# Two row tiles of x: transposed by DMA in place of TensorE

## The chip, the cores and the metric

The kernel runs on one core of a Trainium2 chip. The metric is the device time of one execution in microseconds, and the number to compare is the median of several executions. One further execution is taken with the hardware profiler; every duration, start and wait in this document is from such a profile, with times counted from the start of its span. In the profile PE is TensorE (PEld its weight loads), DVE VectorE, ACT ScalarE, POOL GpSimd, and SP is SyncE, whose queue issues every DMA of this kernel.

## The reference: what is computed

For x of 2048 rows and 1024 columns (bf16) the kernel computes a mix of two branches:

```python
g = sigmoid((x * gate_w).sum(-1))
# branch a: 32 heads of 32, each position attends 8 positions, 2 apart
q, k, v = x @ wqkv
o = softmax(scale * q . k[pos - 2*w], w = 0..7) . v
a = o @ wo
# branch b: gated MLP with mixing over the positions, Fh = 1792
z = gelu(x @ w_in);  z1, z2 = z[:, :Fh], layernorm(z[:, Fh:])
b = (z1 * (w_sp @ z2 + b_sp)) @ w_out
out = g * a + (1 - g) * b
```

Both branches start with a product over the columns of x. TensorE sums over the partition axis, so x is needed with its columns on the partitions: transposed.

## The kernel before

The 2048 rows are 16 tiles of 128 rows. `xT` holds x transposed, 128 partitions by 8 k tiles by 2048 rows, in one arena of SBUF that the whole kernel shares. The kernel goes through these stages, in this order on PE: six warm-up matmuls on zeros; a first block of `z2` (the second half of z) for row tiles 0 and 1 and the first two blocks of 448 columns of `w2`, the part of w_in that z2 needs (32 matmuls, L370); `z2` tiles 2 to 7 for the first block of columns, one more for the second; then the q, k, v projections of head group 0 (16 tiles of 8 matmuls, `qkv_tile`, L938), those of the other seven groups, with further z2 work between them, z1 (L1089), the mixing over the positions, and the two output products (L1106 for all three).

ACT empties the PSUM banks: gelu for z2 (L379), a copy into a staging slot for q, k, v (L941). Every fourth q/k/v tile SP stores the slot to DRAM (L946); there are three slots, so the fourth use of a slot waits for its store. Per head group the attention runs on DVE (L505 to L579), on q, k and v that SP loads back from DRAM in another layout (L587 to L596).

x reaches `xT` in two ways. Row tiles 0 and 1 are loaded as they lie (L915), into `xn`, a part of the arena that the attention uses later; `turn` transposes them on PE, four 128x128 pieces into one PSUM tile (L352), and ACT (L355) or DVE (L357) copies the PSUM tile to `xT`. Row tiles 2 to 15 are loaded by a transposing DMA, which writes straight into `xT` (L919, L922). `x_abs` (L383) sums the absolute values of two row tiles on DVE, for a scale that x is converted with later.

The order on each engine is the order in which the program gives the instructions. At the start that order is written out by hand. Later a planner (`Beat`) counts PE columns as time and puts DVE, ACT and DMA work in at due times; that is fixed when the kernel is built. SP is one queue: at the start it issues, in this order, the two plain x loads, eight loads of `w2` (one per k tile, 224 KB each), six transposed x loads, three loads of wqkv for group 0, eight transposed x loads, some small ones, wqkv for group 1, four loads of another part of w_in, and only then the first stores of q, k, v.

PSUM tiles are given out in turn: `bank()` takes every fourth from a pool of two, the others from a pool of six, from which `turn` takes its four too.

## Time and profile before

| | us |
|---|---|
| median of 3 runs (lowest, highest) | 672.64 (672.32, 672.66) |
| the profiled execution, its own time | 671.37 |
| span of that profile | 669.6 |
| PE busy in the span | 663.5 |
| DVE busy | 575.2 |
| ACT busy | 441.6 |
| moved by DMA | 123.92 MB, 185 GB/s on average |

The profile is of one execution, whose own time is 1.27 us below the median; the span leaves out 1.8 us around it. A busy PE is not a PE at its peak, since matmuls overlap and their ends are modelled. In a line of the timeline the columns are start, duration, engine, line, operation, what is written and read, and in brackets the idle time before it with what ended it. SPq is SP's queue: the duration there is the time that SP needs to issue the DMA, not the transfer.

### The profile page before, as it was taken

The page shows a single profiled execution, that of the slowest core. Times are in us where ns is not written, and L with a number is a line of the kernel's source. Part 1 is how long each engine was busy: PE and PEld are TensorE (multiplying, and loading weights), DVE is VectorE, ACT ScalarE, POOL GpSimd, SP SyncE. Part 2 cuts the span into 40 slices and gives each one's busy share as a digit, 9 for nine tenths or more (in the row PEclk, how much of TensorE's full clock was granted, in tenths as well). Part 3 has the DMA queues.
Part 4 walks back from the last instruction along what each step waited for, and adds up shares of the span by engine and source line. Part 5 has one row for each costly group of instructions (what it writes and reads, how often), then busy time and mean ns, then how long its engine had stood idle before and what let it go on. Part 6 is the DMA issues. An engine that isn't in the chain of part 4 may idle for free.

```text
span 669.6 us, 9598 instructions
## 1 busy us (share of the span) xinstructions
PE 663.5 (99%) x3564; PEld 389.8 (58%) x3564; DVE 575.2 (86%) x660; ACT 441.6 (66%) x774; POOL 9.4 (1%) x68
## 2 busy tenths in 40 slices
PE   9999999999999999999999999999999999999998
PEld 4568876666777777555555455555555544444443
DVE  4667999989999999999999999999978788954745
ACT  4437667788889989889754568777777774522122
POOL 0000000000001000000000000000000000000000
PEclk9999999999999999999999999999999999999999
DMA  8999574354298996994956686648589799476211
GB/s 237 176 246 269 103 203 131 91 121 119 49 278 250 281 303 186 277 342 146 276 209 217 140 216 162 159 123 231 141 209 287 144 242 253 93 159 150 56 63 64
DMA packets 229919, 123.92 MB, mean 185 GB/s; under 512 B 191088, under 2 KB 217456, under 8 KB 229872
## 3 DMA queue, kind: packets, MB, share of 16 engines
q1 hardware_dynamic: 229872, 123.31, 69.8%
q8 instruction: 28, 0.46, 0.3%
q14 instruction: 19, 0.16, 0.1%
HBM read 63.97 MB, written 37.82 MB: 152 GB/s over the span
## 4 chain that ended last, share of the span: by engine, by line
PE 55%; DVE 40%; ACT 3%; issue 2%; DVEq 0%; ACTq 0%
PE ps L1106 36%; DVE arena L509 8%; DVE arena L505 7%; DVE arena L572 7%; PE seed L1106 6%; PE ps L938 6%; DVE arena L578 3%; PE ps L370 2%; DVE arena L801 2%; PE sd L938 2%; DVE arena L579 2%; DVE arena L819 2%; DVE arena L575 1%; DVE att_L L512 1%; PE sd L370 1%
## 5 line engine op out<-in xcount | busy, mean ns | idle before, releaser
L1106 PE MATMUL ps<-arena 128*128 128x448 f16 (+1 forms) x1296 | 263.7, 363 | 0.7 <-ACT arena L1118 0.6
L1106 PEld LDWEIGHTS <-arena 128*128 128x128 f16 x1519 | 148.5, 98 | 155.0 <-issue 1.5
L938 PEld LDWEIGHTS <-arena 128*128 128x128 f16 (+1 forms) x1024 | 141.4, 138 | 30.6 <-issue 1.1
L938 PE MATMUL ps<-arena 128*128 128x384 bf16 x800 | 142.5, 326 | 0.7 <-DVE arena L487 0.7
L1089 PEld LDWEIGHTS <-arena 128*128 128x128 f16 x512 | 50.0, 98 | 46.6
L509 DVE TENSOR_TENSOR arena<-arena 128x4096 bf16<-128x4096 bf16 (+1 forms) x64 | 74.0, 1157 | 1.8
L1089 PE MATMUL ps<-arena 128*128 128x448 bf16 x384 | 75.4, 352 | 0.0
L505 DVE TENSOR_TENSOR arena<-arena 128x8192 bf16<-128x8192 bf16 x16 | 70.8, 4422 | 4.4 <-DMA arena<-k_d 4.1
L572 DVE TENSOR_TENSOR arena<-arena,att_A 128x8192 bf16<-128x8192 bf16 x16 | 70.7, 4420 | 0.2
L941 ACT CAST arena<-ps 128x384 bf16<-128x384 f32 x100 | 47.8, 487 | 29.4 <-PE ps L938 28.7
L1106 PE MATMUL seed<-arena 128*128 128x448 f16 (+2 forms) x223 | 48.7, 360 | 0.0
L370 PE MATMUL ps<-arena 128*128 128x448 bf16 x216 | 45.4, 352 | 0.2 <-ACT arena L355 0.2
L451 PE MATMUL ps<-arena 128*128 128x449 f16 x192 | 42.3, 353 | 0.0
L938 PE MATMUL sd<-arena 128*128 128x384 bf16 x224 | 41.0, 326 | 0.0
L1092 ACT ACTIVATE arena<-ps,x_sc 128x448 bf16<-128x448 f32 x48 | 29.5, 639 | 15.5 <-PE ps L1089 11.9
L1330 ACT ACTIVATE arena<-ps,omr 128x512 f32<-128x512 f32 x24 | 16.5, 687 | 32.7 <-PE ps L1106 32.7
L370 PEld LDWEIGHTS <-arena 128*128 128x128 f16 (+1 forms) x256 | 24.9, 98 | 22.0 <-ACT arena L355 0.5
L578 DVE TENSOR_TENSOR arena<-arena 128x4096 bf16<-128x4096 bf16 x16 | 36.6, 2287 | 0.2
L1264 DVE SCALAR_TENSOR_TENSOR arena<-seed,omr,arena 128x512 bf16<-128x512 f32 x8 | 6.0, 751 | 32.7 <-PE seed L1106 32.7
L451 PEld LDWEIGHTS <-arena 128*128 128x128 f16 x224 | 21.9, 98 | 18.1 <-issue 0.5
L760 ACT ACTIVATE arena<-arena 128x2048 bf16<-128x2048 bf16 x16 | 30.9, 1929 | 0.0
L885 ACT ACTIVATE arena<-arena 128x896 bf16<-128x896 bf16 x32 | 30.3, 947 | 0.5
(190 smaller groups left out, 738.4 us busy)
## 6 DMA issues: line engine op xcount, KB each, us to landing
arena<-in_B_w_sp_dram SPq DMA_DIRECT2D x16, 512.0 KB, 4.1
arena<-v_d SPq DMA_DIRECT2D x8, 960.0 KB, 6.6
z_d<-arena SPq DMA_DIRECT2D x16, 448.0 KB, 4.5
arena<-z_d SPq DMA_DIRECT2D x16, 448.0 KB, 3.6
y_d<-arena SPq DMA_DIRECT2D x16, 448.0 KB, 3.0
arena<-k_d SPq DMA_DIRECT2D x7, 960.0 KB, 7.3
arena<-in_A_wqkv_dram SPq DMA_DIRECT2D x24, 256.0 KB, 4.7
q_d<-arena SPq DMA_DIRECT2D x32, 128.0 KB, 2.5
```

Of the source, the lines that this page charges most:

```text
L370: nc.tensor.matmul(ps[:, 0:N], x[:, kt, i * P:(i + 1) * P], _sub_ap(w2, kt * W2P + ZC * c, [[1, N]]), start=(kt == 0), stop=(kt == KT - 1) ...
L451: nc.tensor.matmul(ps[:, 0:DN - 1], lhsT, v[:, k, 0:DN - 1], start=(first and k == 0), stop=(k == 3), skip_group_check=True)
L505: TT(prod.rearrange("p (w j c) -> p w j c", w=W, j=8, c=C), in0, in1, ALU.mult)
L509: return lambda: TT(pv[:, :, 0:n], pv[:, :, 0:n], pv[:, :, n:2 * n], ALU.add)
L572: TT(prod.rearrange("p (w j d h) -> p w j d h", w=W, j=8, d=DH, h=HG), in0, in1, ALU.mult)
L578: return [(4.4, mul), (2.3, lambda: TT(p3[:, 0:4, :], p3[:, 0:4, :], p3[:, 4:8, :], ALU.add)), (1.2, lambda: TT(p3[:, 0:2, :], p3[:, 0:2, ...
L760: nc.scalar.activation(slot, slot, ACT.Abs, accum_out=l1[:, a:a + 1])
L885: nc.scalar.activation(waste, g_ring[n % 4][:, r], ACT.Abs, accum_out=yl[:, k:k + 1])
L938: nc.tensor.matmul(ps[:, 0:3 * C].rearrange("p (t c) -> p t c", t=3), lhsT, wgt[:, :, kt, :], start=(kt == 0), stop=(kt == KT - 1))
L941: nc.scalar.copy(st[:, j % 4, :].rearrange("p (t d h) -> p t d h", t=3, h=HG), ps[:, 0:3 * C].rearrange("p (t h d) -> p t d h", t=3, h=HG))
L1089: nc.tensor.matmul(ps[:, 0:512 if whole and kt == 0 else ZC], xh[:, kt, i * P:(i + 1) * P], _sub_ap(w1, kt * ZC, [[1, 512 if whole and kt ...
L1106: nc.tensor.matmul(ps[:, 0:c1 - c0], w[:, k, :], v[:, k, c0:c1], start=(first and k == 0), stop=(k == K - 1), skip_group_check=True)
```

## The change

Row tiles 0 and 1 are loaded by a transposing DMA into `xT`, like the others. SP issues tile 0, then the first `w2` load, tile 1, then the other seven `w2` loads. `xn`, `x_v` and `turn` go, and with them 16 transposes, four copies and four PSUM tiles. Nine warm-up matmuls are given instead of six. In the first block the order within each k tile becomes (tile 0, both column blocks), (tile 1, both), where it was (column block 0, both tiles), (column block 1, both).

```diff
-    xn = reg(A_OFF, 2 * D).rearrange("p (i d) -> p i d", i=2)
...
-    x_v = x2.rearrange("(i q) d -> q i d", q=P)
...
-    def turn(i, h):
-        pt = psum.tile([P, 4, P], BF, name="pt", tag="ps")
-        for k in range(4):
-            nc.tensor.transpose(pt[:, k, :], xn[:, i, (4 * h + k) * P:(4 * h + k + 1) * P], ident[:])
-        dst = xT[:, 4 * h:4 * h + 4, i * P:(i + 1) * P]
-        if h == 0:
-            nc.scalar.copy(dst, pt[:])
-        else:
-            nc.vector.tensor_copy(dst, pt[:])
...
-    for i in range(2):
-        sync.dma_start(xn[:, i, :], x_v[:, i, :])
     for kt in range(KT):
+        if kt < 2:
+            sync.dma_start_transpose(xT[:, :, kt * P:(kt + 1) * P], x2[kt * P:(kt + 1) * P, :])
         sync.dma_start(w2[:, kt, :], B_w_in[kt * P:(kt + 1) * P, FH:FH + 2 * ZC])
     for i in range(2, 8):
         sync.dma_start_transpose(xT[:, :, i * P:(i + 1) * P], x2[i * P:(i + 1) * P, :])
...
-    warm_up(6)
-    for i in range(2):
-        for h in range(2):
-            turn(i, h)
-    z2_block([(i, c) for c in range(2) for i in range(2)])
+    warm_up(9)
+    z2_block([(i, c) for i in range(2) for c in range(2)])
     x_abs(0)
```

## The prediction

> **What bounds the kernel now.** I read the totals, then each engine's waits, then SP's own queue from the start of the span. First the page and two lists of waits (engine, line, what it waited for: us in total, times, longest):

> ```profile
> span 669.6 us, 9598 instructions
> PE 663.5 (99%) x3564; PEld 389.8 (58%) x3564; DVE 575.2 (86%) x660; ACT 441.6 (66%) x774; POOL 9.4 (1%) x68
> ...
> PE ps L938 <- DVE arena L487: 0.7, 2, 0.5
> PE ps L1106 <- ACT arena L1118: 0.6, 1, 0.6
> ...
> DVE arena L505 <- DMA arena<-k_d: 4.1, 1, 4.1
> DVE arena L437 <- ACT arena L433: 0.3, 1, 0.3
> ...
> DVE att_m L556 <- ACT att_L L552: 3.0, 1, 3.0
> ```

> PE has no gap worth naming. DVE, between 55 and 372 us, waits only three times in earnest: 4.1 us at 55.55 for the first k_d load, 0.3 at 82.07, 3.0 at 136.26 for an ACT exponential that is timed by PE. And PE itself waits for DVE at 107.25 and 129.12. So two chains run side by side with some 0.3 us between them, and the chain of waits goes along DVE to 371 us and along PE after it. What makes the attention start late at 55.55 reaches the end, less 0.3.

> What sets 55.55? SP's queue (start, us, instruction; then single transposed loads, the last two from later stages; then ACT):

> ```profile
> 0.73 0.88 SPq L915 DMA_DIRECT2D arena<-in_A_x_dram  x2
> 1.65 3.75 SPq L917 DMA_DIRECT2D arena<-in_B_w_in_dram  x8
> 5.45 9.34 SPq L919 DMA_TRANSPOSE arena<-in_A_x_dram  x6
> 14.83 3.17 SPq L345 DMA_DIRECT2D arena<-in_A_wqkv_dram  x3
> 18.05 12.12 SPq L922 DMA_TRANSPOSE arena<-in_A_x_dram  x8
> ...
> 5.45 1.35 SPq L919 DMA_TRANSPOSE arena<-in_A_x_dram  x1
> 6.84 2.53 SPq L919 DMA_TRANSPOSE arena<-in_A_x_dram  x1
> 9.42 1.31 SPq L919 DMA_TRANSPOSE arena<-in_A_x_dram  x1
> 505.04 2.94 SPq L674 DMA_TRANSPOSE arena<-o_d  x1
> 531.93 2.05 SPq L674 DMA_TRANSPOSE arena<-o_d  x1
> ...
> 46.18 0.48 ACT L941 CAST arena<-sd 128x384 bf16<-128x384 f32 x1 [7.56 <-DMA v_d<-arena]
> ```

> SP issues from 0.73 to 46 us without waiting for any engine. Its stores of the first four q/k/v tiles go out only at 37.44, though ACT had finished them by 29; the last of the three (39.61) lands at 46.18 and lets ACT go on, then come the last stores, the k_d load at 51.41, and DVE at 55.55. A microsecond more on SP before 14.83 is a microsecond at 55.55. It also matters what stands ahead of a transposed load: one behind other transposed loads takes 1.31 us of SP, one behind a plain transfer still in flight 2.05 to 2.94, or it takes 1.35 and the next one 2.53.

> **The change part by part.**

> Removed on PE: 16 transposes, 3.71 to 5.48. The next 31 matmuls of the first block run from 5.88 at 0.189 us (8 in 1.51), and the tile behind them starts at 11.75. Removed beside it: two ACT copies (0.58 each), two DVE copies (0.42 each) and four PSUM tiles. ACT is next needed at 11.38 and DVE had idled 3.5 us before the first x_abs that waits for a load (11.81), so the copies are worth nothing beyond the block's start. ACT loads its gelu table earlier, in idle time.

> Added on PE: three warm-up matmuls, 3 x 0.43 (2.57 us for the first six, start to start): they would end at 1.18 + 9 x 0.43 = 5.05 and lie in the wait for x, worth nothing unless tile 1 lands before 5.05.

> SP: two plain loads go (0.92 of SP), two transposed ones come. Start to start: tile 0 1.39 (row 5.45 to 6.84), one w_in tile 0.475 (3.80 for eight), tile 1 1.36 (9.42 to 10.78), seven w_in tiles 3.33, tile 2 1.39, tile 3 1.36 if nothing stalls, tiles 4 to 7 5.41 (9.42 to 14.83). Sum 14.72 against 14.10: SP is late by 0.62, without any stall. With stalls: tile 1 goes right behind a plain load. Its bounds are 0 (the 1.35 row) and +1.63 (2.94 less 1.31, one plain load of 448 KB issued 0.45 us ahead); the row behind y_d stores gives +0.74. The load here is half as long, 224 KB: I take 0.8. Tile 3's stall of 1.22 (2.53 less 1.31) stands in the trace behind eight w_in tiles; afterwards seven stand there, and the loads come slower: between 0 and 1.22, I take 0.9. SP reaches the first wqkv load 0.62 + 0.8 + 0.9 = 2.3 us later, bounds 0.6 and 3.5.

> Queued behind: tiles 2 to 15, the wqkv loads, the q/k/v stores. The wqkv load issued at 16.08 lands 5.7 later, 21.8, and PE wants it at 22.34: 0.55 us of cover. Tiles 2 to 7 land 1.6 to 2 us ahead of PE (x_abs starts on landing: 11.81, while PE takes tile 3 at 13.26). If SP is late by 2.3 and PE by less than 1.75, PE stalls for wqkv; PE's slack for ACT's late copies at 47 us is about 0.7, used up in the same way.

> PE's start: tile 1 is issued at 0.73 + 1.39 + 0.475 = 2.60. Landing takes 3.4 to 3.9 behind transposed loads (12.8 less 9.42 for tile 4), 4.9 to 5.9 behind plain ones (4.9 at 531.93, 5.2 for tile 2). I take 4.9, the nearest in stall: 7.5, bounds 6.0 and 8.5. Two of 32 matmuls can run before it (tile 0 alone); the other 30 take 5.67, so the next tile starts at 13.2 against 11.75: PE +1.5 (0.0 to +2.5). The second w_in tile, issued near 4.8 and landing 3.2 to 3.8 later, can add up to 0.6.

> Sum: DVE's chain +2.3 - 0.3 = +2.0; PE's +1.5 to 2.1, brought to +1.75 by wqkv at least. The later one decides: +2.0 us. The profiled execution is 669.6 of span and 1.8 around it, 671.37, and 1.27 below the median of the runs; I expect 671.6 of span and 672.64 + 2.0 = 674.6 as median.

> [...] Over tiles 2 and 3 the DMA engines moved 274 GB/s (8.2 to 9.4) at full share, over the w_in tiles 363 (6.9 to 8.2). 512 KB more at the lower rate are 1.9 us against 1.4. [...]

> **The rivals.**

> A, no stall: tile 1 passes the single w_in tile as the 1.35 row did, and tile 3's stall goes with the thinner backlog. For it: six of eight w_in tiles were still to come when tile 2 stalled nothing. Against: the 2.05 and 2.94 rows, with little ahead of them. SP +0.6, less 0.3; PE 0.0: 672.9.

> B, a transposed load costs what a plain one costs in SP and transfer, and the exchange is hidden: the shift is 0, 672.6. For it: DMA engines are full until 8.9 either way. Against: 1.31 of SP each time.

> C, faster: tile 1 lands 2.56 after issue, as the first plain x tile did at the latest (0.73 to 3.29), at 5.2, and the block is 0.9 shorter; the stalls at 6.84 (1.22) and 18.05 (2.65 less 1.31) go too, so that SP is early by 0.62 - 2.56 = -1.9 and DVE follows down to PE's -0.9 and the 0.47 that PE waits at 129.12: -1.4, 671.2. PE is early at all only if tile 1 lands before 6.0, and by enough for 0.2% only from about 5.2. Against: no transposed load of the trace lands in under 3.4.

> D, the clock: the transposes run at 106 ns, the matmuls after 5.3 at 0.189 for 448 columns, so PE became fast near 5.2. If a wait of some 2.4 us behind the warm-ups brings it back, 30 matmuls take 0.378 instead of 0.189, +5.7 at most; for half of them +2.8, 1.5 to 2 of it beyond the SP shift: 676.5. Against it: the wait is shorter than the 4.0 us of work that made it fast. [...]

> **How the numbers follow.** Forecast 0.55, its own range 674.0 to 675.9 (shift 1.4 to 3.2). A 0.25, B 0.08, C 0.06, D 0.06. 0.2% is 1.35 us, about what a measurement of this kernel can tell from no change. Slower: forecast and D, 0.61; same: A and B, 0.33; faster: C, 0.06. Leaving out C, D and the tail of the forecast, the range is 672.5 to 675.9.

> **What would show it.** Tile 1's issue at 2.60 taking about 2.1, tile 3's 1.31 to 2.5; the first wqkv load at 17.1 instead of 14.83; the second part of the first block at 7.5; DVE's first L505 at 57.8, still waiting for k_d; the first L1106 matmul at 374.2. Wrong if tile 1 takes 1.31 and lands by 6.3 (then A), if L505 moves less than L345 does, or if DVE finds a wait after 82 us in which the delay is lost.

## The result

The changed kernel takes 674.69 us (median of 7, 673.95 to 675.62), the kernel before 672.36 in the same set (7 runs, 672.10 to 673.11). The ratio is 1.003, with a 95% interval of 1.0020 to 1.0039: slower by 1.3 to 2.6 us. The profiled execution takes 674.69 with a span of 672.8, 3.2 us more than the span of the profile before; that earlier execution, at 671.37, was itself 1.0 us quicker than the 672.36, which is why the profiles are further apart than the medians.

Lines of the changed file are lower by 2 at first, then by 12, and by 15 at the end: L370 became L358, L505 L493, L345 L343, L941 L929, L552 L540. First the span and DVE's waits between 50 and 372 us, as they were shown of before:

```profile
span 672.8 us, 9567 instructions
...
DVE arena L493 <- DMA arena<-k_d: 3.9, 1, 3.9
DVE att_m L544 <- ACT att_L L540: 3.0, 1, 3.0
DVE arena L425 <- ACT arena L421: 0.3, 1, 0.3
```

The same three waits stand there, with the same lengths within 0.2 us (a fourth, of 0.3 us for POOL, is in both profiles): behind 55 us DVE's run is the old one, only later. Now SP's queue of the changed kernel, tile 3's load by itself, then the ACT copy that waits for a store, then DVE's first attention step:

```profile
0.73 1.35 SPq L904 DMA_TRANSPOSE arena<-in_A_x_dram  x1
2.14 0.56 SPq L905 DMA_DIRECT2D arena<-in_B_w_in_dram  x1
2.75 1.25 SPq L904 DMA_TRANSPOSE arena<-in_A_x_dram  x1
4.05 3.42 SPq L905 DMA_DIRECT2D arena<-in_B_w_in_dram  x7
7.52 10.02 SPq L907 DMA_TRANSPOSE arena<-in_A_x_dram  x6
17.59 3.08 SPq L343 DMA_DIRECT2D arena<-in_A_wqkv_dram  x3
...
8.80 3.33 SPq L907 DMA_TRANSPOSE arena<-in_A_x_dram  x1
...
49.48 0.48 ACT L929 CAST arena<-sd 128x384 bf16<-128x384 f32 x1 [7.45 <-DMA v_d<-arena]
...
58.76 4.42 DVE L493 TENSOR_TENSOR arena<-arena 128x8192 bf16<-128x8192 bf16 x1 [3.91 <-DMA arena<-k_d]
```

The first wqkv load leaves 2.76 us later (17.59 for 14.83), ACT goes on 3.30 later, DVE starts 3.21 later, and the span is 3.2 longer. Tile 1 stalled nothing (1.25); tile 3 stalled SP for 3.33, where 2.53 stood before. The first block on PE:

```profile
1.18 3.75 PE L114 MATMUL pw<-arena 128*128 128x512 bf16 x9 [1.18 <-DVE arena L109]
5.14 0.54 PE L358 MATMUL ps<-arena 128*128 128x448 bf16 x2 [0.21 <-DMA arena<-in_B_w_in_dram]
6.25 0.36 PE L358 MATMUL ps<-arena 128*128 128x448 bf16 x1 [0.57 <-DMA arena<-in_A_x_dram]
8.04 1.28 PE L358 MATMUL ps<-arena 128*128 128x448 bf16 x3 [1.24 <-DMA arena<-in_B_w_in_dram]
14.95 4.70 PE L358 MATMUL ps<-arena 128*128 128x448 bf16 x24
```

Tile 1 is there at 6.25, 3.5 us after its issue. But the second w_in tile, issued at 4.05 behind it, lands only at 8.04, and the other 28 matmuls then take 6.9 us where 28 x 0.189 = 5.3 were forecast. The granted clock shows why (columns: stretch, its length, busy time of PE, PEld, DVE, ACT and POOL with instructions, granted clock, share of the DMA engines, GB/s):

```profile
7.60:7.80 0.20, 0.00 (x0) 0.00 (x0) 0.20 (x1) 0.00 (x0) 0.00 (x0) 1.00 1.09 350
7.80:8.00 0.20, 0.00 (x0) 0.00 (x0) 0.20 (x1) 0.00 (x0) 0.00 (x0) 0.85 0.86 332
8.00:8.20 0.20, 0.16 (x1) 0.10 (x1) 0.20 (x1) 0.00 (x0) 0.00 (x0) 0.50 0.85 251
...
11.20:11.40 0.20, 0.20 (x2) 0.04 (x1) 0.00 (x0) 0.00 (x0) 0.00 (x0) 0.62 1.17 178
11.40:11.60 0.20, 0.20 (x3) 0.11 (x2) 0.00 (x0) 0.00 (x0) 0.00 (x0) 1.00 1.22 137
```

The clock falls to half at 7.94 and is back at 11.35 (0.85 and 0.62 are means over the steps). This does not come in every execution: 3.4 us at half lower the mean clock of the span to 0.997, and of the seven executions four have 0.995 to 0.997 on record, the other three 0.999 or 1.000. So the tile behind the block starts at 14.95 instead of 11.75: 1.6 us of it is the later w_in tile (8.04 for 6.45), 1.6 the clock.

PE's first block and DVE's start are both 3.2 us late. Which one makes the end late?

### The profile page after: what moved, and what is told of

Its sections match the earlier page's. It is cut to its first block, busy times and chain, and to the rows that moved or that the text cites. A ratio compares the mean times of both kernels' runs of the same rounds, so it can differ in the third digit from the quotient of the medians.

```text
span 672.8 us, 9567 instructions
## 1 busy us (share of the span) xinstructions
PE 665.0 (99%) x3551; PEld 388.8 (58%) x3551; DVE 574.2 (85%) x658; ACT 439.5 (65%) x771; POOL 9.4 (1%) x68
## 2 busy tenths in 40 slices
DMA packets 231743, 123.92 MB, mean 184 GB/s; under 512 B 193168, under 2 KB 219536, under 8 KB 231696
## 4 chain that ended last, share of the span: by engine, by line
PE 54%; DVE 40%; ACT 3%; issue 2%; DMA 1%; SPq 0%; DVEq 0%; ACTq 0%
PE ps L1091 36%; DVE arena L497 8%; DVE arena L493 7%; DVE arena L560 7%; PE seed L1091 6%; PE ps L926 6%; DVE arena L566 3%; PE ps L358 3%; DVE arena L789 2%; PE sd L926 2%; DVE arena L567 2%; DVE arena L807 2%; DVE arena L563 1%; DVE att_L L500 1%; PE sd L358 1%
## 5 line engine op out<-in xcount | busy, mean ns | idle before, releaser
L1074 PE MATMUL ps<-arena 128*128 128x448 bf16 x384 | 75.4, 353 | 0.0
L493 DVE TENSOR_TENSOR arena<-arena 128x8192 bf16<-128x8192 bf16 x16 | 70.7, 4422 | 4.2 <-DMA arena<-k_d 3.9
L929 ACT CAST arena<-ps 128x384 bf16<-128x384 f32 x100 | 47.7, 485 | 29.7 <-PE ps L926 27.7
L358 PE MATMUL ps<-arena 128*128 128x448 bf16 x216 | 46.8, 360 | 2.0 <-DMA arena<-in_B_w_in_dram 1.5
L358 PEld LDWEIGHTS <-arena 128*128 128x128 f16 (+1 forms) x256 | 25.3, 99 | 25.8 <-issue 4.3
L1077 ACT ACTIVATE arena<-ps,x_sc 128x448 bf16<-128x448 f32 x48 | 29.8, 637 | 15.6 <-PE ps L1074 12.7
L371 DVE TENSOR_REDUCE yl<-arena 128x1 f32<-128x2048 bf16 x8 | 18.2, 2284 | 18.7 <-DMA arena<-in_A_x_dram 18.7
```

What stands on the lines that cost most here:

```text
L358: nc.tensor.matmul(ps[:, 0:N], x[:, kt, i * P:(i + 1) * P], _sub_ap(w2, kt * W2P + ZC * c, [[1, N]]), start=(kt == 0), stop=(kt == KT - 1) ...
L493: TT(prod.rearrange("p (w j c) -> p w j c", w=W, j=8, c=C), in0, in1, ALU.mult)
L929: nc.scalar.copy(st[:, j % 4, :].rearrange("p (t d h) -> p t d h", t=3, h=HG), ps[:, 0:3 * C].rearrange("p (t h d) -> p t d h", t=3, h=HG))
L1074: nc.tensor.matmul(ps[:, 0:512 if whole and kt == 0 else ZC], xh[:, kt, i * P:(i + 1) * P], _sub_ap(w1, kt * ZC, [[1, 512 if whole and kt ...
L1077: nc.scalar.activation(z1s[:, i % 4, :], ps[:, 0:ZC], ACT.Gelu_apprx_tanh, scale=xinv)
```

## The experiments

The theory, E: SP's queue (through the stores and the k_d load to DVE) and PE's first block each carry to the end, and the later decides. Its rivals: only PE counts (P), or only SP (S). All comparisons are with the kernel before, run beside it on the same chip.

**SP late alone.** Kernel before with

```diff
+    for i in range(2):
+        sync.dma_start_transpose(reg(A_OFF + 2048 + 1024 * i, 1024).rearrange("p (k s) -> p k s", k=KT), x2[i * P:(i + 1) * P, :])
     for i in range(2, 8):
         sync.dma_start_transpose(xT[:, :, i * P:(i + 1) * P], x2[i * P:(i + 1) * P, :])
```

> The kernel before with two more transposed loads of x (to a part of the arena that nothing reads) behind the eight w_in loads: SP is later by 2 x 1.36 = 2.7 us, with a stall perhaps up to 1.2 more or less; PE's first block is untouched. Theory E: DVE starts its attention 2.7 late, 0.3 of it is slack: 672.4 + 2.4 = 674.8 (674.0 to 676.0). Rival P: SP's lateness is absorbed on the way, 672.4.

Measured: 675.33 us, ratio 1.0049 (1.0037 to 1.0061). From its timeline:

```profile
17.99 2.97 SPq L345 DMA_DIRECT2D arena<-in_A_wqkv_dram  x3
...
59.15 4.43 DVE L505 TENSOR_TENSOR arena<-arena 128x8192 bf16<-128x8192 bf16 x1 [3.90 <-DMA arena<-k_d]
```

SP is 3.16 late, DVE's start 3.60, the span is 673.4. P falls: without the changed first block the whole loss is there. (PE isn't untouched: tile 2 is late as well, PE waits 2.2 us for it until 13.87, and the clock is then at half from 14.28 to 17.69. At the first q/k/v matmul PE is 3.8 late, 26.15 for 22.34; less the 1.0 of the next run that is 2.8, too little to decide.)

**PE late alone.** Kernel before with

```diff
-    warm_up(6)
+    warm_up(18)
```

> The kernel before with 18 warm-up matmuls instead of 6: 3 of the 12 more at 0.43 us and 9 at 0.216, so the first block starts and ends 3.2 us later; SP is untouched. Theory E: PE's chain is 3.2 late, at most 0.7 of it is slack where PE waits for DVE (107 and 129 us): 672.4 + 2.8 = 675.2 (674.6 to 675.8). A rival S (only SP's queue counts, PE catches up): 672.4.

Measured: 673.69 us, ratio 1.0019 (1.0010 to 1.0027). The first line is of the kernel before, from DVE's timeline; the fence below is of this run, with the tile behind the first block ahead:

```profile
136.26 0.43 DVE L556 TENSOR_TENSOR att_m<-att_L 128x256 f32<-128x256 f32 x1 [3.00 <-ACT att_L L552]
```

```profile
14.96 4.70 PE L370 MATMUL ps<-arena 128*128 128x448 bf16 x24
...
55.60 4.42 DVE L505 TENSOR_TENSOR arena<-arena 128x8192 bf16<-128x8192 bf16 x1 [0.95 <-DMA arena<-k_d]
82.13 2.10 DVE L437 TENSOR_TENSOR arena<-arena 128x1800 f16<-128x1800 f16 x2 [0.33 <-ACT arena L433]
138.48 0.43 DVE L556 TENSOR_TENSOR att_m<-att_L 128x256 f32<-128x256 f32 x1 [5.17 <-ACT att_L L552]
```

The block is as late as in the changed kernel (14.96), DVE starts on time (55.60). DVE goes on as before up to 136 us, where it waits for the exponential on ACT, which PE's progress times; there it is 2.22 late, and the span is 2.3 longer. So PE's lateness does count, but 1.0 us of it is absorbed; 0.7 of that is the length of PE's two waits for DVE at 107 and 129 us, which are gone in this run. S falls too. The forecast of 675.2 missed all the same: by the medians the run costs 1.6 us (0.7 to 1.8), less than by the profiles, whose reference was a quick execution.

One more thing stands in this profile. The first wqkv load leaves 0.86 us late (15.69), though SP's program is the old one, and DVE starts only 0.05 late. So a delay on SP before that load isn't carried to DVE one for one, as the prediction had it.

**The clock held.** Changed kernel with

```diff
-    warm_up(9)
+    warm_up(20)
```

> The changed kernel with 20 warm-up matmuls instead of 9: PE is busy through the wait for the second w_in tile (8.04 us), so the granted clock should stay at 1.00 where it fell to 0.50 from 7.9 to 11.4 us. SP is untouched. Theory E (SP's queue and PE's first block each delay the end, the later one decides; SP alone is 2.8 us late at the first wqkv load and 3.3 at the first stores): the first block ends some 1.0 to 1.6 us earlier and the end hardly moves, 674.4 (674.0 to 674.8). Rival P (PE's late first block carries the loss alone, SP's lateness is absorbed): the clock's 1.6 us come back, 673.1.

Measured: 674.85 us, ratio 1.0037 (1.0024 to 1.0049), as without them. The mean granted clock is 1.00, and the matmuls behind the warm-ups run 0.19 us apart; the tile behind the block starts at 13.47, 1.5 earlier; DVE's start does not move:

```profile
13.47 4.71 PE L358 MATMUL ps<-arena 128*128 128x448 bf16 x24
...
58.96 4.43 DVE L493 TENSOR_TENSOR arena<-arena 128x8192 bf16<-128x8192 bf16 x1 [5.15 <-DMA arena<-k_d]
```

The clock's 1.6 us were lost on PE and cost nothing at the end that these runs can tell. In the changed kernel SP's side decides: 3.2 against PE's 3.2, or 3.4 by the first q/k/v matmul, less 1.0.

**The place of the transposed tiles.** Changed kernel, both tiles ahead of all eight w_in loads:

```diff
-    for kt in range(KT):
-        if kt < 2:
-            sync.dma_start_transpose(xT[:, :, kt * P:(kt + 1) * P], x2[kt * P:(kt + 1) * P, :])
+    for i in range(2):
+        sync.dma_start_transpose(xT[:, :, i * P:(i + 1) * P], x2[i * P:(i + 1) * P, :])
+    for kt in range(KT):
         sync.dma_start(w2[:, kt, :], B_w_in[kt * P:(kt + 1) * P, FH:FH + 2 * ZC])
```

> The changed kernel with both transposed tiles issued ahead of all eight w_in loads. Nothing plain stands ahead of tile 1 and no transposed load among the w_in loads. Theory T (a transposed tile keeps the DMA engines busy for longer than a plain one, whatever its place): the w_in loads are drained at the same time, near 11.2 us, tile 3 is held until then, the first wqkv load comes at 17.6, and the time stays at 674.7 (674.2 to 675.2). Rival O (it is the change from plain to transposed loads and back that costs): one change less, SP about 1 us earlier, 673.7.

Measured: 674.69 us, ratio 1.0032 (1.0020 to 1.0043), the first wqkv load at 17.41, 0.18 us earlier where O wanted 1: T rather than O, though by the time alone O's 673.7 lies just at the lower end of the interval. What a transposed tile does to the DMA engines is seen in three stretches, of the kernel before and then of the changed one (columns as above):

```profile
1.70:6.70 5.00, 4.79 (x28) 2.75 (x27) 1.51 (x4) 2.34 (x4) 0.00 (x0) 1.00 0.97 326
6.70:8.90 2.20, 2.20 (x13) 1.12 (x12) 1.64 (x1) 0.42 (x1) 0.00 (x0) 1.00 1.10 359
8.90:11.20 2.30, 2.30 (x14) 1.19 (x13) 0.00 (x0) 0.00 (x0) 0.00 (x0) 1.00 1.11 223
```

```profile
1.70:6.70 5.00, 4.22 (x13) 1.32 (x12) 0.39 (x1) 0.31 (x1) 0.00 (x0) 1.00 0.90 196
6.70:8.90 2.20, 0.96 (x4) 0.40 (x3) 2.09 (x2) 0.00 (x0) 0.00 (x0) 0.78 0.92 297
8.90:11.20 2.30, 2.30 (x8) 0.88 (x6) 0.00 (x0) 0.00 (x0) 0.00 (x0) 0.50 1.17 335
```

Up to 6.7 us the engines are taken for 0.97 and 0.90 of the time, but move 326 GB/s before and 196 after: 0.65 MB less in 5 us, of which 0.16 in the first 0.8 us, when the engines weren't yet taken. The whole program moves 123.92 MB in both kernels, but with the two tiles transposed in 231,743 packets instead of 229,919, and those under 512 B are 2,080 more. The w_in loads, gone by 8.9 before (the rate falls to 223), still run at 335 GB/s until 11.2. Tile 3's load frees SP at 9.37 before and at 12.13 after, each 0.5 to 0.9 us behind that point. In both kernels, then, SP comes free of tile 3's load only when the w_in loads have drained. It is the same in the ten other runs of this section in which SP issues the w_in loads: in the 0.5 us before the held load frees SP (from 9.8 to 12.7 us) the rate falls to between 13 and 128 GB/s, and behind it the rate is up again. That the drain is what frees SP fits all twelve, but no run shows it by itself.

**As many bytes, plain.** Kernel before with two more plain loads where the first run had two transposed ones:

```diff
+    for i in range(2):
+        sync.dma_start(reg(A_OFF + 2048 + 1024 * i, 1024), x_v[:, i, :])
     for i in range(2, 8):
```

> The kernel before with two more plain loads of x, 256 KB each, behind the eight w_in loads, where the earlier run had two more transposed ones (3.2 us later at the first wqkv load). Theory T (it is the transposing that costs, on SP and in the DMA engines): 2 x 0.44 of SP and 2 x 0.72 us of transfers, the step at 55.55 is 1.0 to 1.5 later, 672.3 + 1.3 = 673.6. Rival B (bytes and descriptors in the queue cost, transposed or not): as late as with the transposed loads, 675.3.

Measured: 674.43 us (673.72 to 676.20), ratio 1.0032 (1.0016 to 1.0048); its profile is of the longest of its executions, with DVE's start 3.68 late where T forecast 1.0 to 1.5. The first wqkv load leaves at 16.66, 1.83 late, against 3.16 with the transposed pair: on SP the transposing makes up 1.3 us. In time the two runs' intervals overlap, so at the end T and B are not told apart; 512 KB of extra transfers cost something either way. Here 1.83 us on SP went with 3.68 at DVE's start, in the run with PE late 0.86 with 0.05: whether it is SP's issuing that makes DVE late, or the time that the transfers themselves take, no run separates.

**w_in from another queue.** Changed kernel, the eight w_in loads issued by ACT:

```diff
-        sync.dma_start(w2[:, kt, :], B_w_in[kt * P:(kt + 1) * P, FH:FH + 2 * ZC])
+        nc.scalar.dma_start(w2[:, kt, :], B_w_in[kt * P:(kt + 1) * P, FH:FH + 2 * ZC])
```

> The changed kernel with its eight w_in loads issued by ACT instead of SP; SP issues the transposed loads one behind another. ACT is idle at that time. SP would be early: 8 x 0.475 = 3.8 less at the first wqkv load, if nothing stalls, so about 1 us earlier than in the kernel before. PE starts when tile 1 and the w_in tiles land, which now share the DMA engines with four tiles of x from the start: first block complete between 11.5 and 13.5 (11.75 before, 14.95 after). Theory E: PE decides, 672.4 to 673.8. Rival P gives the same. If the time stays at 674.7 it is not SP's issue but the transfers that are late.

Measured: 677.02 us, ratio 1.0076 (1.0061 to 1.0091), worse than all the forecasts. SP is not early but 1.74 late (first wqkv load at 16.57): its loads of tiles 2 and 3 take 3.29 and 4.01 us. Nor did ACT's queue get through: the loads that SP issued in 3.75 us take it 12.34, the last four leaving at 3.40, 6.03, 10.54 and 12.71. Tile 1, issued at 2.13, lands only at 10.57:

```profile
0.73 12.34 ACTq L905 DMA_DIRECT2D arena<-in_B_w_in_dram  x8
...
10.57 0.56 PE L358 MATMUL ps<-arena 128*128 128x448 bf16 x1 [3.59 <-DMA arena<-in_A_x_dram]
...
17.84 4.70 PE L358 MATMUL ps<-arena 128*128 128x448 bf16 x24
...
141.34 0.43 DVE L544 TENSOR_TENSOR att_m<-att_L 128x256 f32<-128x256 f32 x1 [5.31 <-ACT att_L L540]
```

With four to six w_in loads issued beside it, and SP's next two transposed loads, the transposed tile takes 8.4 us. What held the two queues isn't shown; the run does not free SP, as was meant. PE is 6.1 late at the block and DVE 5.1 late at 136 us: again 1.0 absorbed, and here PE decides.

**Stores ahead of later loads.** The first stores of q, k, v stand behind seven loads on SP. Kernel before, changed kernel, and changed kernel with 20 warm-ups, each with

```diff
-    load_wg(1)
-    for q in range(4):
-        load_d(q)
...
         qkv_tile(0, j)
+        if j == 3:
+            load_wg(1)
+        if j == 7:
+            for q in range(4):
+                load_d(q)
```

> The kernel before, with the loads of wqkv for group 1 issued behind the first q/k/v stores and the four later w_in loads behind the second, instead of all seven ahead of the first: the stores leave some 5 us earlier, ACT should not wait for the store at 46 us, and DVE's attention starts 2 to 4 us earlier. Theory E with the slack that the late-PE run showed (3.2 us on PE became 2.2 at 136 us, so PE has 1.0 of slack): PE decides now, and the end comes 0.7 to 1.0 earlier, 671.3. If PE's own chain had no slack, 672.1; if DVE's start alone counted, 669.

> The changed kernel with the same reordering of the stores: SP's lateness no longer decides. PE's does, 3.2 us at the first block and 3.4 at the first q/k/v matmul, less 1.0 of slack: 672.13 + 2.3 = 674.4 (674.0 to 674.7). So the store order alone should win only some 0.3 here. If SP's lateness were the whole loss: 671.5.

> The changed kernel with the reordering and 20 warm-ups: neither alone should help much, both together should. PE is 1.7 late at the first block and 2.4 at the first q/k/v matmul (it waits there for wqkv), less 1.0: 672.13 + 1.4 = 673.5 (673.0 to 673.9). If the time stays at 674.4 or more, the clock was not what made PE late; if it falls to 672 or below, PE's lateness is absorbed altogether.

Measured: 672.11 us for the first, ratio 0.9992 (0.9980 to 1.0003), which can't be told from the kernel before; 673.58, 1.0017 (1.0007 to 1.0028), and 673.85, 1.0016 (1.0005 to 1.0026). ACT no longer waits for the store, but DVE's start hardly moves: 54.95 in the first, 58.85 and 58.15 in the others. The four loads of 448 KB now stand right ahead of the last stores, which DVE needs as much; the wait was moved. So these runs don't test PE's slack, and the forecast that DVE would start 2 to 4 us earlier was wrong. They are about a microsecond better than the changed kernel (0.3 was forecast for the first of the two), with intervals that overlap, and the warm-ups again make no difference.

**The four loads behind DVE's loads.** Kernel before, and changed kernel with 20 warm-ups, with

```diff
     load_wg(1)
-    for q in range(4):
-        load_d(q)
...
+    for q in range(4):
+        load_d(q)
     t0 = beat.now
     for q in range(4):
-        beat.at(t0 + 1.0 + 2.4 * q, lambda q=q: d_norm(q))
-    beat.at(t0 + 9.0, d_total)
+        beat.at(t0 + 8.0 + 2.4 * q, lambda q=q: d_norm(q))
+    beat.at(t0 + 16.0, d_total)
```

> The kernel before, with the four later w_in loads (4 x 448 KB) issued behind the loads of q and k for group 0 instead of ahead of the first stores, and their norms 7 us later in ACT's order. 3.0 us of SP and 1.8 MB of transfers go from ahead of DVE's first attention step to behind it. Theory E: that step (55.55) starts 3 us or more earlier, PE decides with its 1.0 of slack: 672.3 - 1.0 = 671.3 (670.9 to 671.7). If the step starts earlier and the end does not move, PE has no slack and the reading of the late-PE run is wrong: 672.3.

> The changed kernel with the same four loads moved behind, and 20 warm-ups, so that neither SP's lateness nor the clock should decide any more. PE is left: 1.7 late at the first block, 2.4 at the first q/k/v matmul where it waits for wqkv, less 1.0 of slack: 672.3 + 1.4 = 673.7 (673.0 to 674.0), against 674.7 for the changed kernel. If it is no better than 674.4, PE's start was the loss after all.

Measured: 675.35 us, 1.0044 (1.0031 to 1.0057), and 677.00, 1.0063 (1.0049 to 1.0077): both slower. From the first:

```profile
52.99 4.43 DVE L505 TENSOR_TENSOR arena<-arena 128x8192 bf16<-128x8192 bf16 x1 [0.90 <-DMA arena<-k_d]
...
69.75 0.19 PE L427 MATMUL ps<-rs_n,rs_b 128*128 128x1 bf16 x1 [2.76 <-DVE rs_n L422]
69.80 5.45 PE L936 MATMUL ps<-arena 128*128 128x384 bf16 x24
```

DVE starts 2.56 us earlier, as meant, but PE now reaches the matmul that needs the total of the norms before DVE has it, and waits 2.76 (3.27 in the other). Within the wait the clock falls: it is at half from 69.22 to 72.64, and the 24 matmuls behind, with 3.94 us to the next tile in the kernel before, take 5.29. PE is then 4.95 late (75.09 for 70.14), DVE 3.96 late at 136 us, and the span 4.0 longer; in the other run it is 6.87, 5.87 and 5.9. So 1.0 us is absorbed here too, but a new wait took more than the old one gave, and PE's slack stays without a test from the side of a gain. A further version that put off the steps behind the norms as well computes something else, and its time is not used. No version beat the kernel before.

Over the single profiles the account can be checked (us later than in the profile before; the first column is PE's lateness at the first q/k/v matmul, in the last two rows behind the new wait, at 75 and 77 us; the second is the first less PE's slack):

| run | PE | less 1.0 | DVE's first step | span |
|---|---|---|---|---|
| changed kernel | 3.4 | 2.4 | 3.2 | 3.2 |
| 20 warm-ups | 2.4 | 1.4 | 3.4 | 3.4 |
| tiles first | 3.5 | 2.5 | 2.7 | 2.7 |
| SP late | 3.8 | 2.8 | 3.6 | 3.8 |
| PE late | 3.2 | 2.2 | 0.1 | 2.3 |
| w_in from ACT | 6.1 | 5.1 | 2.8 | 5.1 |
| stores ahead, before | 0.2 | -0.8 | -0.6 | -0.6 |
| stores ahead, changed | 2.5 | 1.5 | 3.3 | 3.3 |
| the same, 20 warm-ups | 3.1 | 2.1 | 2.6 | 2.6 |
| plain loads more | 1.4 | 0.4 | 3.7 | 4.8 |
| four loads behind, before | 5.0 | 4.0 | -2.6 | 4.0 |
| four loads behind, changed | 6.9 | 5.9 | -1.0 | 5.9 |

In eleven of twelve rows the span follows the larger of the second and third columns within 0.2 us. In the row of the plain loads PE also waits 2.10 us for DVE at 110.93; why the end is 1.1 later than DVE's start there wasn't followed up.

## Why the prediction came true, and where it did not

The forecast was a shift of 2.0 us to 674.6; the medians differ by 2.3. The path held: the loads late on SP's side, the delay carried by the stores and the k_d load to DVE's start, and from there to the end. That the number is so near is in part luck, since several terms were wrong and offset each other. Step by step:

- **SP's sum.** Forecast 2.3 at the first wqkv load, measured 2.76. The base of 14.72 was right to 0.2 (16.86 from 0.73 to 17.59, less tile 3's stall of 2.02, plus 0.06 by which tile 1 was quicker: 14.9). Two terms were mis-sized. Tile 1's stall, 0.8 forecast, was nothing (1.25 in all): the rows of 2.05 and 2.94 did not apply to a plain load issued so early. Tile 3's, 0.9, was 2.02: I let it shrink with seven w_in loads ahead instead of eight, while these, issued behind the two transposed tiles, drained 2.3 us later (11.2 for 8.9). The terms' errors offset each other. Single profiles also scatter here: with the same SP program up to that load, the kernel before and three of its variants issue it at 14.83, 15.37, 15.51 and 15.69, the changed kernel and four variants at 16.94 to 18.16. The profile before is the earliest of its four, and between the medians of the two groups lie 2.2 us.
- **The sign for rival A.** The prediction called itself wrong, and A right, if tile 1 took 1.31 us and landed by 6.3. It took 1.25 and landed by 6.25, so the sign spoke for A. A's 672.9 didn't come, because A also needed tile 3's stall to go, and that grew. The sign tested one stall of the two.
- **From SP to DVE.** Later by another 0.5 than forecast (2.76 to 3.21): the eight transposed loads behind wqkv took 12.89 us of SP instead of 12.12, which no term foresaw. The sentence that a microsecond before 14.83 is one at 55.55 is too simple, as the runs with 0.86 and 1.83 us show.
- **The 0.3 us of slack at 82 us.** There is none: the wait is 0.33 whether DVE comes 0, 0.1, 3.2 or 3.6 late, since the ACT step it waits for is started by DVE. The forecast subtracted it wrongly; 3.21 at 55.55 is 3.2 at the end.
- **Tile 1's landing.** Forecast 7.5 from the rows behind plain loads, measured 6.25, near the lower bound of 6.0. Its place as the late one was taken by the second w_in tile, 4.0 us behind its issue (8.04), a term of "up to 0.6" that came to 1.4 (6.63 would have been its turn).
- **The clock, rival D.** Held unlikely, and it came: 0.50 from 7.94 to 11.35. The forecast waited for a single gap and compared it with the 4.0 us that it took to become fast; that a gap has to be as long was the author's estimate, and the runs show otherwise. Four matmuls stood in the 3.1 us between the warm-ups and 8.04, and the clock fell all the same; at single gaps of the kind it reckoned with, 2.17 to 2.76 us, it fell in three other profiles. Here the fall cost PE 1.6 us and, as the run with 20 warm-ups shows, the end nothing, because PE's 3.2 less 1.0 of slack stays below DVE's 3.2. D as priced (676.5) did not happen. The forecast gave PE's chain no slack in its sum; four runs show 1.0.
- **Transposed as fast as plain, rival B.** The measured time is 2.1 above its 672.6. On SP a tile of 256 KB took 1.35 and 1.25 us transposed, where the plain load before took 0.42 and 0.40, and 196 GB/s stand against 326 with the engines taken for 0.90 and 0.97 of the time.
- **The reference execution.** From profile to profile the shift is 3.2, not 2.0. The medians agree with the forecast the better because the profile before was of a quick execution, which is luck; the sum was short by 1.2 of its own measure.

## What to carry to other kernels

Price a transposed load by what it takes of its queue and of the DMA engines (here 1.25 to 1.35 us of SP for 256 KB where nothing held it, against 0.40 to 0.42 plain, and 196 GB/s up to 6.7 us against 326), and look at what stands behind it, not only at the engine work it saves: sixteen transposes and four copies went, and none of that time was on the path that decided. Where two chains run side by side, delay each by itself with work that costs nothing else; one run each told the slack here: 0 and 1.0 us, where the waits read beforehand had given 0.3 and 0.7. A wait of constant length that moves along with its waiter is no slack.
